# Four coupled edits to the order and the VectorE work of a two-kind attention stack on one Trainium2 core

## The chip, the cores and the metric

The kernel runs on one core of a Trainium2 chip. The metric is the time of one execution on the device in microseconds. TensorE (PE in the profile, its weight loads PEld), VectorE (DVE), ScalarE (ACT), GpSimd (POOL) and SyncE (SP, which here only issues DMAs) each run their own queue of instructions in order and wait for one another through semaphores.

## The reference

Four residual blocks on one sequence of 2048 rows by 512 columns, 32 heads of 16:

```python
def _A_ref(x, wqkv, wo):
    qkv = (x @ wqkv).reshape(B, S, 3, H, Dh).transpose(2, 0, 3, 1, 4)
    q, k, v = qkv[0], qkv[1], qkv[2]
    p = softmax(einsum("bhqd,bhkd->bhqk", q, k) * Dh ** -0.5)
    return einsum("bhqk,bhkd->bhqd", p, v).transpose(0, 2, 1, 3).reshape(B, S, D) @ wo

def _B_ref(x, wqkv, w_phi, wo):          # linear attention: phi has two softmaxes over 16
    ...
    num = einsum("bhqf,bhfd->bhqd", phi_q, kv)
    den = einsum("bhqf,bhf->bhq", phi_q, z)[..., None] + 1e-6
    return (num / den).transpose(0, 2, 1, 3).reshape(B, S, D) @ wo

x = x + _A_ref(layernorm(x), A_wqkv, A_wo)
x = x + _B_ref(layernorm(x), B_wqkv, B_w_phi, B_wo)
x = x + _A_ref(layernorm(x), A_wqkv, A_wo)
x = x + _B_ref(layernorm(x), B_wqkv, B_w_phi, B_wo)
```

The change concerns the two softmax attentions (`_A_ref`), called the first and the second attention here.

## The kernel before

**Groups, steps and tiles.** An attention is 32 groups: a group is four heads (`g`) and 512 queries (`j`). A group has 16 steps, one per 128 keys. A step needs two score tiles of 128 x 1024 (two heads each). `scores` (L1165 through `score_cols`) writes one into one of two PSUM buffers `s`; ScalarE exponentiates it into `p` (L1172), which has six buffers. When both tiles of a step are there, `pvs` (L1215) multiplies them with the values and adds into the group's accumulators, a pair of PSUM banks. There are two such pairs: `double` and `pm`. The other pair serves everything else that TensorE does on the side: projections for the next heads, output products, transposes for the next layer.

**End of a group.** `norm_task` empties the pair by two 32x32-block transposes on VectorE (`turned_sum`, L864, into tiles `yt` and `yb`), GpSimd adds the two halves (L867), VectorE takes the reciprocals (`rec`, L935 and L937) and scales (L942). Only the transposes keep the pair full. The names `vyt` are the same two transposes for values of later heads, `tq` (L887, L889) are queries and keys. `yt`, `vyt` and `tq` share one ring, the tag `yt`, of three tiles. A `vyt` tile leaves for the value buffer `v` by 16 DMAs on SP's queue (L877), and its slot is free when they have landed.

**An octet** is eight heads. While one octet is attended to, the values, queries and keys of the next are made: four value tiles, then eight query and key tiles, whose squares (`sq`, L982, on GpSimd) give norms; their maximum over all partitions is a GpSimd reduction (`nma`, L917) from VectorE's `nmx` (L914), and from it GpSimd computes a shift row `sh` and a check value `okt` (L921).

**Exponentials on VectorE.** Some score tiles do not go to ScalarE. `power_task` computes their exponential as a polynomial with VectorE: four instructions that empty the pair (L1183, L1186, into `px` and `pw`), and for each half a shift (L1192), a square `z = w * w` on GpSimd (`pz`, L1195) and four multiply-adds (L1197 to L1203). There is one buffer for such a tile (`px`). In the kernel before, it is always the second tile of a group's last step, at most one per group, and taken only after the group before has been finished.

**What sets the order.** The order on all compute engines is written out when the kernel is built. The loop in `attention` walks along TensorE's time by a table of costs (`UNIT` for a score tile or a side piece, `STEP` for a step's products, `EXP`, `THERE`, `BACK`) and picks what comes next: a score tile when a PSUM buffer and a `p` slot are due, a step's products, or a side piece. `Plan` keeps a clock for VectorE ("V") and GpSimd ("P"); tasks are generators that say which engine they need, for how long, and with which rank (lower first; 1 where none is given). `advance` gives each engine the due task of the lowest rank. These costs decide the order only; on the chip each queue runs when its waits are over. DMAs stand on SP's queue in the order in which tasks issue them.

At the end of the program VectorE and GpSimd reduce `okt` to a flag (`lowest` L1806, `bad` L1808, `anybad` L1810, `flag` L1812) that chooses a fallback; these four float to an earlier place in the queues.

## Time and profile before

| what | value |
|---|---|
| time, median of 3 runs (lowest to highest) | 2559.85 us (2557.07 to 2563.15) |
| profiled execution: its time, its span | 2557.37 us, 2555.6 us |
| mean granted TensorE clock | 0.983 |
| busy: PE, PEld, DVE, ACT, POOL | 2324.0, 1090.4, 1548.2, 2134.2, 633.0 us |
| first attention, from its first to past its last exponential | 71 to 1040 us |
| second attention | 1351 to 2305 us |

The rows of a group of instructions read: line, engine, operation, output<-inputs, shapes, count, then busy time and the mean of one in ns, then the idle time of the engine just before them with what ended most of it. Lines of waits read: who waited <- for whom: total us, times, longest. Timeline lines read: start and length in us, engine, line, operation, and in brackets the idle time before it. A wait for several semaphores is put down to the one that came last. SPq is SP's queue.

### The profile page before, as it was taken

How to read it: one execution, taken by the hardware profiler on the slowest of the kernel's cores; microseconds unless marked ns; L12 is line 12 of the kernel's file. 1: busy time of each engine (PE TensorE's matmuls, PEld its weight loads, DVE VectorE, ACT ScalarE, POOL GpSimd, SP SyncE). 2: the span in 40 equal slices, each digit the busy share in tenths (PEclk: the TensorE clock that was granted, in tenths of full speed). 3: DMA queues.
4: the chain of work that ended last, by engine and by line, in shares of the span. 5: the costliest groups of instructions: out<-in, count | busy, mean ns of one | idle time of the engine just before them, and what ended most of it. 6: DMA issues, size and time to landing. Idle time of an engine off the chain costs nothing.

```text
span 2555.6 us, 103557 instructions
## 1 busy us (share of the span) xinstructions
PE 2324.0 (91%) x46698; PEld 1090.4 (43%) x46698; DVE 1548.2 (61%) x2731; ACT 2134.2 (84%) x2382; POOL 633.0 (25%) x733
## 2 busy tenths in 40 slices
PE   6989999999989999899889999999899899998998
PEld 4434444444434444445344444444344344444543
DVE  8256556755556356789961565665465532468897
ACT  6889999999999999544438999999999999994553
POOL 3112211221121000366431122212122110005552
PEclk9999999999999999999899999999999999999999
DMA  5310331141036321000133003212300531110003
GB/s 194 64 26 7 74 63 33 51 56 43 3 93 167 127 85 60 26 17 17 67 102 55 16 16 46 39 24 35 58 3 11 94 110 61 61 68 26 9 18 109
DMA packets 114925, 142.86 MB, mean 56 GB/s; under 512 B 64184, under 2 KB 69928, under 8 KB 112168
## 3 DMA queue, kind: packets, MB, share of 16 engines
q1 hardware_dynamic: 113288, 133.38, 20.9%
q8 instruction: 367, 6.01, 1.0%
q0 software_dynamic: 1184, 2.77, 0.3%
q14 instruction: 86, 0.70, 0.1%
HBM read 62.16 MB, written 41.94 MB: 41 GB/s over the span
## 4 chain that ended last, share of the span: by engine, by line
ACT 44%; PE 24%; DVE 13%; issue 11%; SPq 5%; POOL 2%; DMA 1%; ACTq 0%; DVEq 0%; POOLq 0%
ACT p L1172 42%; PE double L1215 5%; PE s L1165 4%; SPq L877 3%; PE pm L699 2%; PE pm L1215 2%; PE pbv L1509 2%; DVE su L1579 1%; PE pk L1509 1%; PE po L682 1%; PE pq L1509 1%; SPq L1152 1%; DVE f L1571 1%; PE double L699 1%; DVE f L1572 1%
## 5 line engine op out<-in xcount | busy, mean ns | idle before, releaser
L1172 ACT ACTIVATE p<-s 128x1024 f32<-128x1024 f32 x2004 | 1851.4, 1067 | 72.5 <-PE s L1165 70.4
L1165 PE MATMUL s<-kq 49*32 49x512 f16 x15168 | 788.6, 382 | 103.4 <-ACT p L1172 90.4
L1165 PEld LDWEIGHTS <-kq 49*32 49x32 f16 x15872 | 386.8, 90 | 893.9 <-issue 822.6
L1215 PE MATMUL double<-p,v 64*32 64x512 f32 x10768 | 737.7, 591 | 12.1 <-DVE yt L864 6.3
L1215 PE MATMUL pm<-p,v 64*32 64x512 f32 x5264 | 359.9, 592 | 0.0
L867 POOL TENSOR_TENSOR yt<-yt,yt 128x512 f32<-128x512 f32 x64 | 83.5, 1304 | 772.4 <-DVE yt L864 719.5
L1215 PEld LDWEIGHTS double<-p,v 64*32 64x32 f32 x10768 | 207.9, 106 | 52.8 <-issue 13.7
L864 DVE STREAM_TRANSPOSE yt<-double 128x512 f32<-128x512 f32 x86 | 57.6, 698 | 222.5 <-PE double L1215 211.4
L1509 PEld LDWEIGHTS <-xnTa 128*128 128x128 f16 x1152 | 111.5, 99 | 156.9 <-DVE f L1572 28.1
L982 POOL TENSOR_TENSOR sq<-stg 128x512 bf16<-128x512 f16 x48 | 57.6, 1199 | 389.9 <-PE s L1165 278.6
L1588 POOL TENSOR_TENSOR f<-f,su 128x1024 f32<-128x1024 f32 x62 | 119.9, 1934 | 131.8 <-DVE su L1582 105.5
L1195 POOL TENSOR_TENSOR pz<-pw 128x512 f32<-128x512 f32 x88 | 99.6, 1137 | 92.4 <-DVE pw L1186 45.3
L1509 PE MATMUL pbv<-wbv,xnTa 128*128 128x512 f16 x384 | 95.4, 401 | 23.4 <-DVE f L1572 23.4
L1249 DVE SCALAR_TENSOR_TENSOR xt<-pm,c_oA,xt 128x512 f32<-128x512 f32 x68 | 50.5, 743 | 107.9 <-PE pm L699 105.8
L1573 ACT ACTIVATE f<-f,c_pB 128x1024 f32<-128x1024 f32 x64 | 72.7, 1148 | 50.4 <-DVE f L1572 50.3
L1197 DVE SCALAR_TENSOR_TENSOR px<-pz,px 128x512 f32<-128x512 f32 x88 | 78.8, 895 | 58.5 <-POOL pz L1195 51.6
L1215 PEld LDWEIGHTS pm<-p,v 64*32 64x32 f32 x5264 | 101.8, 106 | 17.8 <-DVE yt L864 1.8
L699 PEld LDWEIGHTS <-wA 64*32 64x32 f16 x4608 | 75.8, 93 | 42.2 <-issue 4.1
L1594 ACT ACTIVATE fk<-f 128x1024 f16<-128x1024 f32 x30 | 31.7, 1057 | 72.7 <-POOL f L1588 72.7
L864 DVE STREAM_TRANSPOSE vyt<-pm 128x512 f32<-128x512 f32 x46 | 30.2, 692 | 96.6 <-PE pm L699 83.5
L1509 PE MATMUL pq<-wbqk,xnTa 128*128 128x512 f16 x384 | 88.4, 379 | 0.0
L1509 PE MATMUL pk<-wbqk,xnTa 128*128 128x512 f16 x384 | 88.1, 379 | 0.0
(319 smaller groups left out, 3073.1 us busy)
## 6 DMA issues: line engine op xcount, KB each, us to landing
kq<-stg SPq DMA_DIRECT2D x168, 128.0 KB
xd<-xt SPq DMA_DIRECT2D x40, 512.0 KB
xt<-xd SPq DMA_DIRECT2D x40, 512.0 KB
v<-vyt SPq DMA_DIRECT2D x384, 16.0 KB
oD<-osp SPq DMA_DIRECT2D x24, 256.0 KB
ob<-oD SPq DMA_DIRECT2D x8, 768.0 KB
xt<-in_A_x_dram SPq DMA_DIRECT2D x8, 512.0 KB
wbqk<-dBqk SPq DMA_DIRECT2D x2, 2048.0 KB
```

The lines of the kernel that those rows point to most:

```text
L699: nc.tensor.matmul(ps[h][c, :], w[r, c], x[r], start=(n == 0), stop=(n == of - 1), skip_group_check=True)
L864: nc.vector.transpose(ys[u].rearrange("p a b -> p (a b)"), ps[u])
L867: nc.gpsimd.tensor_tensor(ys[0], ys[0], ys[1], ALU.add)
L877: nc.sync.dma_start(dst[:, :, 33 * a + 1:33 * a + 33], yt[32 * a:32 * a + 32, m:16:4, :])
L1165: nc.tensor.matmul(banks2[u][32 * c:32 * c + 32, :], self.side(g, half, 64 * u, 0, kt * P + 32 * c, 32), self.side(g, half, 64 * u, 1, j * ...
L1172: nc.scalar.activation(pt, s, AF.Exp, scale=EXPS)
L1195: nc.gpsimd.tensor_tensor(z, w, w, ALU.mult)
L1197: nc.vector.scalar_tensor_tensor(y, z, PB, y, op0=ALU.add, op1=ALU.mult)
L1215: nc.tensor.matmul(acc[h][32 * hh:32 * hh + 32, :], self.oct[o]["v"][r, x:x + 32], pt[r, hh % 2, :], start=(kt == 0), stop=(kt == NT - 1), ...
L1509: nc.tensor.matmul(dst, xnT[:, a, c, t * P:(t + 1) * P], w(b, c), start=(i == 0 and c == 0), stop=(i == 2 and c == NC4 - 1))
L1573: nc.scalar.activation(f, f, AF.Exp, scale=con["pB"])
L1588: nc.gpsimd.tensor_tensor(f3, f3, self.part_sums(f3, slice(0, 64), factor), ALU.mult)
```

## The change

- The transposes at a group's end get rank -1, and their task is announced one step's cost earlier. `advance` keeps an engine free for a task of negative rank that would become ready while another instruction runs.
- The square of the polynomial runs on VectorE, so that `power_task` uses no GpSimd.
- Any step's second tile may go to VectorE: the candidate is the second tile `LEAD` = 8 steps ahead of the next score tile. It is taken when the one `px` buffer and an accumulator pair are free, VectorE is booked for at most `VBUSY` = 0.4 us beyond now, the present group has at least three steps of products left, and its keys have landed by the plan (`landed`). It holds for groups 1 to 25.
- The ring `yt` gets four tiles, the ring `sq` four instead of five.
- Constants that set the order: `UNIT` 0.22 to 0.217, `STEP` 0.865 to 0.864, `THERE` 0.53 to 0.54, `BACK` 1.1 to 1.11, `POWERS` 24 to 26.

```diff
+LEAD = 8
+REST = 0.0
+VBUSY = 0.4
...
                     at = max(c, t.ready)
+                    for first in mine:
+                        if rank(first) < 0 and rank(t) >= 0 and max(c, first.ready) < at + t.need[1]:
+                            t, at = first, max(c, first.ready)
...
-        def turned_sum(self, idx, ps, name):
+        def turned_sum(self, idx, ps, name, rank=0):
...
-                yield "V", 0.68, 0
-                ys.append(np_.tile([P, 16, 32], F32, tag="yb" if u else "yt", name=name + str(u), bufs=2 if u else 3))
+                yield "V", 0.68, rank
+                ys.append(np_.tile([P, 16, 32], F32, tag="yb" if u else "yt", name=name + str(u), bufs=2 if u else 4))
...
-            yt = yield from self.turned_sum(idx, acc, "yt")
+            yt = yield from self.turned_sum(idx, acc, "yt", -1)
...
-                yield "P", 1.0
+                yield "V", 0.69, 2
                 z = new("pz")
-                nc.gpsimd.tensor_tensor(z, w, w, ALU.mult)
+                nc.vector.tensor_tensor(z, w, w, ALU.mult)
...
+                                if kt == NT - 1:
+                                    pvdone = G + 1
+                                    self.spawn(self.norm_task(G, idx, banks2), STEP + 0.3)
                                 pe += STEP
...
-                                if kt == NT - 1:
-                                    pvdone = G + 1
-                                    self.spawn(self.norm_task(G, idx, banks2))
                                 break
-                        if turn == 0 and tiles:
-                            G, kt, h = tiles[0]
-                            if tried < G and 0 < G < POWERS and pvdone >= G and kt <= 9 and min(self.pfree) <= pe and G in acc and pe + UNIT <= max(due, free):
-                                tried = G
-                                npow += 1
+                        if turn == 0 and tiles and pxfree <= pe and rested <= pe and plan.clock["V"] <= pe + VBUSY:
+                            n = NT * tiles[0][0] + tiles[0][1] + LEAD
+                            G, kt = n // NT, n % NT
+                            if 0 < G < POWERS and self.groups[G][0] in self.kq and plan.now >= self.landed[self.groups[G][0]] and pvq[0][0] in acc and \
+                               NT - pvq[0][1] >= 3 and min(self.pfree) <= pe and pe + UNIT <= max(due, free):
+                                power.add((G, kt, 1))
+                                pxfree, rested = FAR, pe + REST
                                 idx, ps = self.take()
-                                self.score_cols(*self.groups[G], NT - 1, 1, ps)
+                                self.score_cols(*self.groups[G], kt, 1, ps)
```

Lines behind the edits have other numbers in the changed kernel: L864, L867, L914, L935 and L1195 are L870, L873, L920, L941 and L1201 there.

What the change does to the queues, at three places. The first is VectorE's queue early in the first attention, from the third value tile of the second octet to the first tile of its keys (`tq`); `yt0_...` empties the accumulators of group 1. The brackets name what an instruction waits for; eight `DMAHW` names are the DMAs of a value tile that hold the ring's slot. Before:

```order
L864 STREAM_TRANSPOSE vyt0_1967<-pm0_1710 128x512 [waits DVE_49,PE_49]
L864 STREAM_TRANSPOSE vyt1_1969<-pm1_1711 128x512 [waits DMAHW4_49,DMAHW3_49,DMAHW5_49,DMAHW2_49,DMAHW6_49,DMAHW1_49,DMAHW7_49,DMAHW0_49,PE_49]
L864 STREAM_TRANSPOSE vyt0_2298<-pm0_1982 128x512 [waits DMAHW4_49,DMAHW3_49,DMAHW5_49,DMAHW2_49,DMAHW6_49,DMAHW1_49,DMAHW7_49,DMAHW0_49,PE_49]
L864 STREAM_TRANSPOSE vyt1_2300<-pm1_1983 128x512 [waits PE_49]
L887 TENSOR_SCALAR tq_2627<-pm0_2313,c_qk_359 128x512 [waits DMAHW4_49,DMAHW3_49,DMAHW5_49,DMAHW2_49,DMAHW6_49,DMAHW1_49,DMAHW7_49,DMAHW0_49,PE_49]
L889 SCALAR_TENSOR_TENSOR tq_2627<-pm1_2314,c_qk_359,tq_2627 128x512 [waits DVE_49,PE_49]
L864 STREAM_TRANSPOSE yt0_2641<-double_1907 128x512 [waits DMAHW3_49,DMAHW4_49,DMAHW2_49,DMAHW5_49,DMAHW1_49,DMAHW6_49,DMAHW0_49,DMAHW7_49,PE_49,Pool_49]
```

In the changed kernel, where a polynomial (sixteen rows, left out here) stands between the third and the fourth value tile:

```order
L870 STREAM_TRANSPOSE vyt0_2419<-pm0_2126 128x512 [waits PE_49]
L870 STREAM_TRANSPOSE vyt1_2440<-pm1_2127 128x512 [waits PE_49]
L870 STREAM_TRANSPOSE yt0_2610<-double_1871 128x512 [waits DMAHW4_49,DMAHW3_49,DMAHW5_49,DMAHW2_49,DMAHW6_49,DMAHW1_49,DMAHW7_49,DMAHW0_49,PE_49]
L870 STREAM_TRANSPOSE yt1_2639<-double_1871 128x512 [waits Pool_49]
L893 TENSOR_SCALAR tq_2683<-pm0_2453,c_qk_359 128x512 [waits DMAHW4_49,DMAHW3_49,DMAHW5_49,DMAHW2_49,DMAHW6_49,DMAHW1_49,DMAHW7_49,DMAHW0_49,PE_49]
```

The fourth value tile (`vyt0_2298` before, `vyt0_2419` now) waits for no DMA, and the emptying of group 1 stands ahead of the `tq` and waits for the DMAs of the first value tile instead of the third.

The second place is behind the reduction `nma` of the third octet in the first attention (values and keys for the third octet are made while the second is attended to). VectorE before:

```order
L914 TENSOR_REDUCE nmx_11427<-nm_7950 128x1 [waits DVE_49]
L1203 SCALAR_TENSOR_TENSOR px_11240<-pw_11273,px_11240 128x512 [waits DVE_49]
L1192 TENSOR_SCALAR px_11240<-px_11240 128x512
L1197 SCALAR_TENSOR_TENSOR px_11240<-pz_11579,px_11240 128x512 [waits DVE_49,Pool_49]
L1199 SCALAR_TENSOR_TENSOR pz_11579<-pw_11295,pz_11579 128x512 [waits DVE_49]
L1201 SCALAR_TENSOR_TENSOR px_11240<-pz_11579,px_11240 128x512 [waits DVE_49]
L1203 SCALAR_TENSOR_TENSOR px_11240<-pw_11295,px_11240 128x512 [waits DVE_49]
L864 STREAM_TRANSPOSE vyt0_11724<-double_11418 128x512 [waits PE_49]
```

VectorE now, up to the first instruction of the next polynomial:

```order
L920 TENSOR_REDUCE nmx_11579<-nm_7889 128x1 [waits DVE_49]
L870 STREAM_TRANSPOSE yt0_11677<-double_11011 128x512 [waits PE_49]
L870 STREAM_TRANSPOSE yt1_11706<-double_11011 128x512
L941 TENSOR_SCALAR rec_11786<-yt0_11677 128x16 [waits Pool_49]
L943 RECIPROCAL rec_11786<-rec_11786 128x16 [waits DVE_49]
L948 TENSOR_TENSOR yn_8984<-yt0_11677,rec_11786 128x16x16 [waits DVE_49]
L956 STREAM_TRANSPOSE yb_11839<-yn_8984 128x512 [waits DVE_49]
L959 CAST osp_11852<-yb_11839 128x512 [waits DMAHW7_49,DVE_49]
L870 STREAM_TRANSPOSE vyt0_11875<-pm0_11581 128x512 [waits PE_49]
L870 STREAM_TRANSPOSE vyt1_11885<-pm1_11582 128x512 [waits PE_49]
L1189 TENSOR_SCALAR px_11908<-pm0_11898 128x512 [waits PE_49]
```

GpSimd at the same place, before and now (an ISA row without names stands ahead of the reduction and again ahead of the next tensor instruction):

```order
L917 ISA nma_11438<-nmx_11427 128x1 [waits DVE_49]
L1195 ISA
L1195 TENSOR_TENSOR pz_11579<-pw_11295 128x512 [waits Pool_49]
L996 MEMSET sh_11600 1x512 [waits DMAHW6_49]
L921 TENSOR_SCALAR okt_134<-nma_11438 1x1 [waits Pool_49]
```

```order
L923 ISA nma_11591<-nmx_11579 128x1 [waits DVE_49]
L873 ISA
L873 TENSOR_TENSOR yt0_11677<-yt0_11677,yt1_11706 128x512 [waits DVE_49]
L1002 MEMSET sh_11780 1x512 [waits DMAHW6_49,Pool_49]
L927 TENSOR_SCALAR okt_134<-nma_11591 1x1 [waits Pool_49]
```

The instruction behind the reduction on GpSimd was the polynomial's square and is now the sum of a finished group's halves; VectorE's `rec` waits for it where `px` did. The same exchange stands behind the reductions of the third and fourth octet in the second attention.

The third place is VectorE behind the last reduction of the second attention, where the program's flag has floated to. Before:

```order
L1197 SCALAR_TENSOR_TENSOR px_41487<-pz_41754,px_41487 128x512 [waits DVE_49,Pool_49]
L1806 TENSOR_REDUCE lowest_51803<-okt_134 32x1 [waits Pool_49]
L1199 SCALAR_TENSOR_TENSOR pz_41754<-pw_41578,pz_41754 128x512 [waits DVE_49]
L1808 TENSOR_SCALAR bad_51805<-lowest_51803 32x1 [waits DVE_49]
L1201 SCALAR_TENSOR_TENSOR px_41487<-pz_41754,px_41487 128x512 [waits DVE_49]
L1203 SCALAR_TENSOR_TENSOR px_41487<-pw_41578,px_41487 128x512 [waits DVE_49]
L1812 CAST flag_51809<-anybad_51807 32x1 [waits Pool_49]
L864 STREAM_TRANSPOSE yt0_41957<-double_41431 128x512 [waits PE_49]
```

Now:

```order
L920 TENSOR_REDUCE nmx_41903<-nm_38607 128x1 [waits DVE_49]
L870 STREAM_TRANSPOSE yt0_41967<-double_41343 128x512 [waits PE_49]
L870 STREAM_TRANSPOSE yt1_41990<-double_41343 128x512
L1818 TENSOR_REDUCE lowest_51861<-okt_134 32x1 [waits Pool_49]
L1820 TENSOR_SCALAR bad_51863<-lowest_51861 32x1 [waits DVE_49]
L1189 TENSOR_SCALAR px_42012<-double_42003 128x512 [waits PE_49]
```

The group's transposes stand ahead of `lowest` and of the flag now, and a polynomial's first instruction stands behind `lowest`.

More of the change, by code (lines that the diff above doesn't have):

```diff
@@ L51 @@
 FAR = 1e9
[L52 to L53 removed]
+UNIT = 0.217
+STEP = 0.864
 EXP = 0.904
[L55 to L57 removed]
+THERE = 0.54
+BACK = 1.11
+POWERS = 26
+LEAD = 8
+REST = 0.0
+VBUSY = 0.4
 LATE = 0.15
@@ L1360, in attention @@
                 plan.add(extra[1], 0.0)
+            self.landed = {0: 0.0, 1: 40.0}
             def pairs(g):
@@ L1364, in pairs @@
                 self.load_pairs(g)
+                self.landed[g] = plan.now + 16.0
             events = []
@@ L1375, in attention @@
             pe = act = 0.0
-            tried = -1
-            npow = 0
+            power, pxfree, rested = set(), 0.0, 0.0
             lost = 0.0
@@ L1465, in attention @@
             assert not plan.tasks and not events
-            print("attention", self.li, "powers", npow, round(pe, 1), "exponentials", len(estart), "late", round(lost, 1), "ready", self.ready)
+            print("attention", self.li, "powers", len(power), round(pe, 1), "exponentials", len(estart), "late", round(lost, 1), "ready", self.ready)
             self.fill.append(self.last_tail(NJ - 1, self.last))
```

23 lines of the change are left out of this document (10 added, 13 removed).

## The prediction

> **What bounds the kernel now.** I read the head of the page, its chain and the line of the exponentials first, then the busy time of each engine in the two attention stretches, then the waits. In the group line the last part is the idle time of ScalarE in front of these instructions and what ended it; in the two lines of stretches the columns are the length, then the busy time of PE, PEld, DVE, ACT and POOL.
>
> ```profile
> span 2555.6 us, 103557 instructions
> ACT 44%; PE 24%; DVE 13%; issue 11%; SPq 5%; POOL 2%; DMA 1%; ACTq 0%; DVEq 0%; POOLq 0%
> L1172 ACT ACTIVATE p<-s 128x1024 f32<-128x1024 f32 x2004 | 1851.4, 1067 | 72.5 <-PE s L1165 70.4
> 71.00:1040.00 969.00, 898.60 (x21460) 409.34 (x21464) 532.14 (x960) 926.66 (x1002) 163.99 (x155) 0.99 0.26 62
> 1351.00:2305.00 954.00, 882.63 (x21373) 400.48 (x21367) 482.79 (x843) 924.72 (x1002) 161.82 (x148) 1.00 0.21 46
> ACT p L1172 <- PE s L1165: 70.4, 65, 7.5
> ```
>
> The two attentions are 1923 of 2556 us, and ScalarE's exponentials fill 96 and 97% of them. An exponential costs 1851.4 / 2004 = 0.924 us. What is left is 70.4 us in which ScalarE waits, 65 times, for TensorE to deliver scores. TensorE runs its queue in order, so whatever holds TensorE up shows there. VectorE is half idle (437 and 471 us). The change acts on these stretches alone; the rest of the span has the same instructions. It can therefore gain by fewer exponentials and by shorter waits, at most 72.5 us for the latter. I looked up what ended the largest ones.
>
> Ring of transposed tiles: the windows 138 to 152 and 592 to 600 (who waited for whom: total, times, longest).
>
> ```profile
> 108.36 35.49 SPq L877 DMA_DIRECT2D v<-vyt  x48
> 134.40 0.75 DVE L887 TENSOR_SCALAR tq<-pm,c_qk 128x512 f32<-128x512 f32 x1 [10.64 <-DMA v<-vyt]
> 145.28 0.72 DVE L864 STREAM_TRANSPOSE yt<-double 128x512 f32<-128x512 f32 x1 [8.90 <-DMA v<-vyt]
> PE double L1165 <- DVE yt L864: 7.7, 1, 7.7
> ACT p L1172 <- PE s L1165: 9.1, 3, 7.5
> ...
> DVE tq L887 <- DMA v<-vyt: 4.4, 1, 4.4
> ACT p L1172 <- PE s L1165: 4.0, 2, 3.3
> ```
>
> A value tile leaves by 16 DMAs, 35.49 / 3 = 11.8 us of SP's queue, and holds its slot of the ring until the last has landed. With three slots VectorE stands in front of the next `yt` or `tq`, an accumulator pair stays full, TensorE waits for it, and ScalarE loses 9.1 and 4.0 us.
>
> GpSimd's square in the polynomial: window 1540 to 1564, and the totals.
>
> ```profile
> 1543.35 0.15 DVE L914 TENSOR_REDUCE nmx<-nm 128x1 f32<-128x4 f32 x1
> 1547.36 0.38 POOL L917 PARTITION_ALL_REDUCE nma<-nmx  x1 [5.83 <-issue]
> 1554.55 1.03 POOL L1195 TENSOR_TENSOR pz<-pw 128x512 f32<-128x512 f32 x1 [6.82 <-issue]
> 1555.62 0.69 DVE L1197 SCALAR_TENSOR_TENSOR px<-pz,px 128x512 f32<-128x512 f32 x1 [10.40 <-POOL pz L1195]
> PE pm L699 <- DVE vyt L864: 2.7, 2, 2.5
> ACT p L1172 <- PE s L1165: 2.8, 1, 2.8
> ...
> DVE px L1197 <- POOL pz L1195: 51.6, 6, 13.5
> ```
>
> After the cross-partition maximum GpSimd does nothing for 6.82 us, and before it 5.83; its next tensor instruction starts 11.1 us after `nmx`. VectorE waits 10.4 us for the square, the transposes of a value tile queue behind it, and TensorE waits for their accumulators. Windows 1727 to 1744 and 1981 to 1986 show the same chain, the second with the end-of-kernel flag (L1812) behind it as well; in 520 to 536 a like wait costs ScalarE next to nothing, since nothing urgent is queued behind it:
>
> ```profile
> ACT p L1172 <- PE s L1165: 4.3, 2, 3.2
> ...
> DVE px L1197 <- POOL pz L1195: 8.6, 1, 8.6
> ACT p L1172 <- PE s L1165: 0.4, 1, 0.4
> ...
> 1981.82 0.14 DVE L1812 CAST flag<-anybad 32x1 int32<-32x1 f32 x1 [5.85 <-POOL anybad L1810]
> ACT p L1172 <- PE s L1165: 2.4, 1, 2.4
> ```
>
> Group boundaries: an ordinary one, and who waits for L864.
>
> ```profile
> 1653.38 1.31 DVE L864 STREAM_TRANSPOSE yt<-double 128x512 f32<-128x512 f32 x2 [6.42 <-PE double L1215]
> 1654.84 1.09 PE L1215 MATMUL double<-p,v 64*32 64x512 f32 x16 [0.17 <-PE pm L699]
> 1656.26 4.69 ACT L1172 ACTIVATE p<-s 128x1024 f32<-128x1024 f32 x5 [0.64 <-PE s L1165]
> ...
>   PE double L1215: 211.4, 37
>   PE pm L1215: 75.2, 16
> ...
>   PE double L1215: 6.3, 6
> ```
>
> While the two transposes empty the pair, TensorE fills in other work and then has two steps to catch up; ScalarE loses 0.64 us. The named waits sum to 9.1 + 4.0 + 2.8 + 4.3 + 2.4 = 22.6; the other 57 waits hold 70.4 - 22.6 = 47.8 us, 0.84 each, most of them such boundaries.
>
> **The change part by part.**
>
> *Tiles anywhere.* The order has 96 `pz` rows instead of 88: 48 tiles for VectorE instead of 44. Four exponentials fewer are 4 x 0.924 = 3.7 us. Ends: 0 and 3.7.
>
> *Longer ring.* At the first place of the order shown above, the change puts `yt0_2610`, which empties group 1, ahead of the `tq` and on the slot of the first value tile. That tile's sixteen DMAs are issued by 108.36 + 11.8 = 120.2, 14 us before even the `tq` of before starts; the wait of 8.9 us has nothing left. Around 595 the `tq` that waited falls on a `yt` slot, free by then. I take 9.1 + 4.0 = 13.1. Ends: 0 (SP's queue is no shorter, and the wait only moves on) and 13.1.
>
> *Polynomial without GpSimd.* The waits of 2.8, 4.3 and 2.4 us can't occur in that form: 9.5 us. Ends 0 and 9.5. The square itself moves to VectorE: 96 instructions. The trace has no such product there; the nearest rows are these, all of 128x512 f32.
>
> ```profile
> L1195 POOL TENSOR_TENSOR pz<-pw 128x512 f32<-128x512 f32 x88 | 99.6, 1137 | 92.4 <-DVE pw L1186 45.3 <-issue 37.8 <-DVE rec L935 5.9
> L647 DVE TENSOR_TENSOR yn<-yt,rec 128x512 f32<-128x512 f32 x32 | 22.7, 711 | 0.0
> L1197 DVE SCALAR_TENSOR_TENSOR px<-pz,px 128x512 f32<-128x512 f32 x88 | 78.8, 895 | 58.5 <-POOL pz L1195 51.6 <-DVE px L1192 0.5
> L1199 DVE SCALAR_TENSOR_TENSOR pz<-pw,pz 128x512 f32<-128x512 f32 x88 | 64.8, 737 | 2.5
> ```
>
> By 0.711 us (between 0.711 and 0.895) that is 68 us, and four more tiles of 10.9 us (below) are 44: 112 us into 908 us of idle VectorE. On the path: nothing, as long as a tile is ready when its step comes (third rival).
>
> *What takes the GpSimd slot.* The reductions stay. At three of them (third octet of the first attention, third and fourth of the second) the order now has the `yt` sum of a finished group right behind the reduction on GpSimd, where `pz` stood, and VectorE's `rec` waits for that sum, with value transposes or a score tile behind it. At the third, VectorE's `lowest` waits for `okt`, which comes after that sum. So a wait of some 5 to 10 us returns at three places. The waits of before that were 8.6 us and longer cost ScalarE between 0.4 and 4.3 us; I take 3 each, 9 us, nearer to those with an emptying behind them, as here. Ends: 3 x 0.4 = 1 and 3 x 4.3 = 13.
>
> *Transposes first.* They start the moment the pair is full at 37 + 16 = 53 of 64 boundaries already; rank can only help the other eleven, by a VectorE instruction of about 0.7 us or two, and TensorE waited directly 6.3 us in six places. By the order the next group takes the same pair at 48 of 62 boundaries (44 before), so the 1.31 us of transposing itself stays. A score tile for VectorE no longer always fills a group's last step, which eases some boundaries more. I take 10 of the 47.8 us, nearest to the 6.3 that the trace shows. Ends: 0 and 47.8. What VectorE idles while it holds itself free for a transpose lies in its idle half.
>
> *The rest.* `sq` with four slots instead of five: a set of four is consumed before the next is written, 0. The DMAs are the same ones, a few places earlier or later on SP, 0. The new constants only set the order.
>
> Sum, against the profiled execution of 2557.4: -3.7 - 13.1 - 9.5 + 9 - 10 = -27.3, so 2530. That execution lies 2.5 us under the median of the runs, 2559.9; beside the median the forecast is **2532 us**. TensorE is idle for 70 us of each stretch, so taking some 14 us from each does not make it the bound.
>
> **The rivals.**
>
> *More of it* (0.16): the three new waits fall where nothing urgent is queued, like that in 520 to 536, and the boundaries give 20: -3.7 - 22.6 + 1 - 20 = -45, 2512, or 2514 beside the median. For it: the boundaries hold 47.8 us. Against it: they keep their 1.31 us.
>
> *The waits change hands* (0.17): the new waits cost 13, and the boundaries give nothing, since the transposes were in time at 53 of 64: -3.7 - 22.6 + 13 = -13, 2544, or 2547 beside the median.
>
> *Late polynomials, slower* (0.10): a tile's place used to be the last step of its group, taken many steps ahead; now it is 8 steps after the start. A step lasts 969 / 512 = 1.89 us, and the products trail by about two tiles: some 17 us of room. A polynomial needs 4 x 0.68 + 2 x (0.50 + 0.71 + 0.74 + 0.74 + 0.72 + 0.71) = 10.9 us from these rows and those above:
>
> ```profile
> L1183 DVE TENSOR_SCALAR px<-pm 128x512 f32<-128x512 f32 x60 | 40.5, 675 | 5.4 <-PE pm L1165 5.2
> L1186 DVE SCALAR_TENSOR_TENSOR pw<-px,pm 128x512 f32<-128x512 f32 x60 | 40.7, 679 | 1.1
> L1192 DVE TENSOR_SCALAR px<-px 128x512 int32<-128x512 int32 x88 | 44.2, 502 | 0.0
> L1201 DVE SCALAR_TENSOR_TENSOR px<-pz,px 128x512 f32<-128x512 f32 x88 | 63.7, 724 | 2.7
> L1203 DVE SCALAR_TENSOR_TENSOR px<-pw,px 128x512 f32<-128x512 f32 x88 | 62.7, 713 | 2.8
> ```
>
> VectorE's other work is (532 - 22 x 9.5) / 969 = 33%, so 5.6 of the 17 us: 16.5 needed. If the tiles come late, TensorE stands in front of them. The gain of 27 is gone at 27 / 48 = 0.57 us per tile; at 1 us the time is 2532 + 48 = 2580. Against it: a tile is only started when VectorE is nearly free, and the exponentials' six slots cover part of a wait. [...]
>
> *It does not do what it says* (0.07): only the four tiles change hands: 2556.
>
> **How the numbers follow.** The forecast has 0.50, its own range 2520 to 2543. The range that should hold 8 of 10 reaches from the first rival to just short of the fourth: 2512 to 2557. A measurement of this kernel tells about 0.2%, 5 us, from no change. Faster: 0.50 + 0.16 + 0.13 of the second rival = 0.79; same: its other 0.04 and the fourth = 0.11; slower 0.10.
>
> **What would show it.** Exponentials 2000; ScalarE's idle time in front of them near 45 us instead of 72.5; no VectorE wait on `v<-vyt` over 3 us at the first octet; no `px` wait on GpSimd, but three `rec` or `lowest` waits of 4 to 10 us behind a reduction, with a ScalarE gap of about 3 us each. TensorE waiting for `px` (L1209) at several tiles would show the slow rival. The forecast is wrong if the attentions are not shorter by 10 to 17 us each, or if the time comes from elsewhere.

## The result, and the profile after

The changed kernel takes 2528.11 us (median of four runs, 2526.15 to 2529.67) against 2558.46 us before (2556.27 to 2563.15): a ratio of 0.9879, 95% interval 0.9861 to 0.9896, or 31 us less (27 to 36). (A fourth run of the kernel before stands beside the three of the first table, so its median is 2558.46 here.) The forecast was 2532, with 2512 to 2557 as its range. The profiled execution took 2528.14 us.

Head of the page of the changed kernel, its chain, the group line of the exponentials, its two attention stretches (from the first exponential to the end of the last one) and ScalarE's largest wait:

```profile
span 2526.1 us, 103429 instructions
ACT 51%; PE 20%; DVE 13%; issue 12%; POOL 3%; SPq 1%; DMA 1%; ACTq 0%; POOLq 0%; DVEq 0%
L1178 ACT ACTIVATE p<-s 128x1024 f32<-128x1024 f32 x2000 | 1846.5, 1068 | 47.6 <-PE s L1171 46.1
71.00:1025.90 954.90, 893.63 (x21456) 410.22 (x21455) 557.51 (x1020) 925.11 (x1001) 114.03 (x111) 1.00 0.27 63
1338.70:2275.50 936.80, 880.81 (x21360) 400.19 (x21359) 528.09 (x935) 921.30 (x999) 113.98 (x104) 1.00 0.22 47
ACT p L1178 <- PE s L1171: 46.1, 55, 4.8
```

The span is 29.5 us shorter. Four exponentials fewer are 3.7 us, and ScalarE's idle time in front of the others has gone from 72.5 to 47.6 us, 24.9 less: 28.6 of the 29.5. By the same measure the attentions took 968.5 and 953.0 us before: they are 13.6 and 16.2 us shorter, and the rest of the span is 634 us as it was. VectorE works 25 and 45 us more in them, GpSimd 50 and 48 us less, and neither is the bound.

What VectorE waits for in the changed kernel (waits of the whole span; then single rows of its timeline at the four places named below, with the idle time ahead in brackets):

```profile
DVE rec L941 <- POOL yt L873: 39.5, 20, 7.0
DVE lowest L1818 <- POOL okt L927: 7.3, 1, 7.3
DVE tq L893 <- DMA v<-vyt: 6.0, 2, 3.4
...
429.31 0.38 POOL L345 PARTITION_ALL_REDUCE sAo_mm<-sAo_m  x1 [5.85 <-issue]
437.12 1.25 POOL L873 TENSOR_TENSOR yt<-yt,yt 128x512 f32<-128x512 f32 x1 [7.43 <-issue]
438.40 0.17 DVE L941 TENSOR_SCALAR rec<-yt 128x16 f32<-128x16 f32 x1 [7.01 <-POOL yt L873]
530.14 0.47 DVE L941 TENSOR_SCALAR rec<-yt 128x16 f32<-128x16 f32 x1 [6.26 <-POOL yt L873]
1728.99 0.47 DVE L941 TENSOR_SCALAR rec<-yt 128x16 f32<-128x16 f32 x1 [1.93 <-POOL yt L873]
```

No `px` waits for GpSimd any more. The waits on `v<-vyt` are down to 6.0 us from 26.6 + 11.1 = 37.7, as these rows of the kernel before have it:

```profile
DVE tq L887 <- DMA v<-vyt: 26.6, 3, 11.5
DVE yt L864 <- DMA v<-vyt: 11.1, 2, 8.9
```

In their place `rec` waits for the sum of a group's halves, where that sum stands behind a reduction on GpSimd: the reduction at 429 is followed by 7.43 us in which GpSimd does nothing, then by the sum. Two of these waits reach ScalarE (windows 430 to 445 and 526 to 540):

```profile
ACT p L1178 <- PE s L1171: 6.6, 3, 4.8
PE pm L1171 <- DVE tq L895: 4.8, 1, 4.8
...
ACT p L1178 <- PE s L1171: 5.2, 4, 3.3
PE pm L1171 <- DVE vyt L870: 3.4, 2, 3.1
```

The other two, around 1729 and the `lowest` at 1961, cost ScalarE 1.4 and 1.2 us in their windows, not more than an ordinary boundary or two.

### The profile page after: what moved, and what is told of

It is laid out like the page before. It is cut to its first block, busy times and chain, and to the rows that moved or that the text cites. A ratio compares the mean times of both kernels' runs of the same rounds, so it can differ in the third digit from the quotient of the medians.

```text
span 2526.1 us, 103429 instructions
## 1 busy us (share of the span) xinstructions
PE 2314.9 (92%) x46698; PEld 1090.1 (43%) x46698; DVE 1618.7 (64%) x2883; ACT 2129.0 (84%) x2378; POOL 535.2 (21%) x645
## 3 DMA queue, kind: packets, MB, share of 16 engines
q1 hardware_dynamic: 113288, 133.38, 21.5%
## 4 chain that ended last, share of the span: by engine, by line
ACT 51%; PE 20%; DVE 13%; issue 12%; POOL 3%; SPq 1%; DMA 1%; ACTq 0%; POOLq 0%; DVEq 0%
ACT p L1178 49%; PE s L1171 4%; PE double L1221 4%; PE pm L1221 2%; DVE su L1591 2%; PE pm L702 2%; PE po L685 1%; PE pbv L1521 1%; PE pk L1521 1%; POOL f L1600 1%; DVE f L1583 1%; SPq L883 1%; DVE f L1584 1%; DVE mx L1580 1%; PE pq L1521 1%
## 5 line engine op out<-in xcount | busy, mean ns | idle before, releaser
L1178 ACT ACTIVATE p<-s 128x1024 f32<-128x1024 f32 x2000 | 1846.5, 1068 | 47.6 <-PE s L1171 46.1
L1221 PE MATMUL double<-p,v 64*32 64x512 f32 x8984 | 617.1, 592 | 2.4 <-DVE yt L870 1.1
L1221 PE MATMUL pm<-p,v 64*32 64x512 f32 x7016 | 479.6, 589 | 0.3 <-issue 0.3
L873 POOL TENSOR_TENSOR yt<-yt,yt 128x512 f32<-128x512 f32 x64 | 87.4, 1365 | 863.2 <-DVE yt L870 809.3
L1221 PEld LDWEIGHTS double<-p,v 64*32 64x32 f32 x8984 | 175.0, 106 | 32.1 <-PE pm L702 3.8
L1221 PEld LDWEIGHTS pm<-p,v 64*32 64x32 f32 x7016 | 136.0, 106 | 24.6 <-issue 2.2
L870 DVE STREAM_TRANSPOSE yt<-double 128x512 f32<-128x512 f32 x72 | 47.3, 696 | 131.5 <-PE double L1221 131.5
L1255 DVE SCALAR_TENSOR_TENSOR xt<-pm,c_oA,xt 128x512 f32<-128x512 f32 x52 | 38.9, 748 | 100.3 <-PE pm L702 87.5
L1255 DVE SCALAR_TENSOR_TENSOR xt<-double,c_oA,xt 128x512 f32<-128x512 f32 x60 | 44.8, 747 | 89.4 <-PE double L702 88.7
L1591 DVE TENSOR_REDUCE su<-f 128x64 f32<-128x1024 f32 x64 | 77.5, 1211 | 9.5 <-ACT f L1585 8.9
L1203 DVE SCALAR_TENSOR_TENSOR px<-pz,px 128x512 f32<-128x512 f32 x96 | 74.0, 771 | 2.7
```

What stands on the lines that cost most here:

```text
L873: nc.gpsimd.tensor_tensor(ys[0], ys[0], ys[1], ALU.add)
L1178: nc.scalar.activation(pt, s, AF.Exp, scale=EXPS)
L1203: nc.vector.scalar_tensor_tensor(y, z, PB, y, op0=ALU.add, op1=ALU.mult)
L1221: nc.tensor.matmul(acc[h][32 * hh:32 * hh + 32, :], self.oct[o]["v"][r, x:x + 32], pt[r, hh % 2, :], start=(kt == 0), stop=(kt == NT - 1), ...
L1255: nc.vector.scalar_tensor_tensor(xt[:, u, :], ps[h], con["oA"], xt[:, u, :], op0=ALU.mult, op1=ALU.add)
L1591: nc.vector.tensor_reduce(su, f[:, r, :], AX.X, ALU.add)
```

## The experiments

All were timed beside the kernel before on the same chip; the ratios are to it. To compare them on one scale I multiply ratios with 2558.5 us: a difference between two ratios of 0.001 is 2.6 us, and a difference of two kernels from different comparisons is uncertain by 5 to 6 us. "Idle" is ScalarE's idle time in the group line of the exponentials. "Long" is the part of it in waits of 2.3 us or more, with those of 0.9 us or more within the 6 us behind them; "rest" is what remains. The three come from one profiled execution of each kernel.

| kernel | median us | ratio (95%) | exps | idle | long | rest |
|---|---|---|---|---|---|---|
| before | 2558.46 | 1 | 2004 | 72.5 | 21.5 | 51.0 |
| changed | 2528.11 | 0.9879 (0.9861 to 0.9896) | 2000 | 47.6 | 9.2 | 38.4 |
| e1 ring alone | 2547.64 | 0.9944 (0.9930 to 0.9957) | 2004 | 62.7 | 13.3 | 49.4 |
| e2 ring undone | 2549.12 | 0.9954 (0.9941 to 0.9968) | 2000 | 76.0 | 34.5 | 41.5 |
| e3 square on GpSimd | 2573.34 | 1.0049 (1.0035 to 1.0063) | 2000 | 90.9 | 53.6 | 37.3 |
| e4 sums on VectorE | 2513.49 | 0.9813 (0.9800 to 0.9826) | 2000 | 34.7 | 0.0 | 34.7 |
| e5 polynomial alone | 2550.97 | 0.9958 (0.9941 to 0.9974) | 2005 | 64.6 | 19.9 | 44.7 |
| e6 ranks undone | 2538.64 | 0.9907 (0.9891 to 0.9924) | 1998 | 53.4 | 12.0 | 41.4 |
| e7 old places | 2534.06 | 0.9892 (0.9875 to 0.9909) | 2004 | 49.6 | 0.0 | 49.6 |
| e8 sums booked | 2520.50 | 0.9840 (0.9822 to 0.9858) | 1999 | 37.2 | 4.1 | 33.1 |
| e9 old places, GpSimd square | 2552.58 | 0.9959 (0.9944 to 0.9973) | 2004 | 68.4 | 12.4 | 56.0 |
| e10 ring and polynomial | 2536.82 | 0.9903 (0.9886 to 0.9920) | 2005 | 56.8 | 10.9 | 45.9 |
| e11 LEAD 9 | 2541.54 | 0.9915 (0.9898 to 0.9932) | 2002 | 58.0 | 18.7 | 39.3 |
| e12 LEAD 9, sums on VectorE | 2520.65 | 0.9856 (0.9831 to 0.9880) | 2002 | 38.1 | 2.4 | 35.7 |

### The ring

e1, on the kernel before (the order stays as it was; `sq` goes to four slots as in the change):

```diff
-  ... tag="yb" if u else "yt", ..., bufs=2 if u else 3)
+  ... tag="yb" if u else "yt", ..., bufs=2 if u else 4)
-  tq = np_.tile([P, 512], F32, tag="yt", name="tq", bufs=3)
+  tq = np_.tile([P, 512], F32, tag="yt", name="tq", bufs=4)
```

> The kernel before with the longer ring of transposed tiles alone (four yt slots, four sq slots). The order of every queue stays as it was; only the slots differ. Theory (the ring's waits are a term of their own, 13 us): VectorE's waits of 8.9 and 4.4 us on the DMAs of value tiles go, ScalarE's idle time in front of the exponentials falls from 72.5 to about 59 us, the time by 11 to 13 us (ratio 0.995). Rival (SP's queue is no shorter, so the wait only moves one tile on): less than 3 us.

14.3 us less (11 to 18), slightly above the theory's 11 to 13. ScalarE's waits at 148 (7.5 and 1.1 us) and 598 (3.3) are gone, and VectorE waits 2.2 us for `v<-vyt` in all where it waited 37.7. ScalarE's idle time fell by 9.8 us only, to 62.7 where 59 was expected: the long waits of the second attention are 13.3 us now, 3.7 more than before.

e2, on the changed kernel, the same lines with 3 for 4.

> The changed kernel with three yt slots again, order unchanged. Theory: the group's transposes come first now and wait about 2 us for the second value tile, the first tq then waits some 10 us for the third; 5 to 13 us slower than the changed kernel, 2533 to 2541 us. Rival (the ring only matters in the order of before): at most 3 us slower.

19 us more than the changed kernel, above both expectations. Waits of VectorE, then of TensorE, in the whole span of e2:

```profile
DVE tq L893 <- DMA v<-vyt: 18.4, 2, 9.8
DVE vyt L870 <- DMA kq<-sh: 8.8, 1, 8.8
DVE yt L870 <- DMA v<-vyt: 6.0, 1, 6.0
PE pm L1171 <- DVE tq L893: 16.5, 3, 8.1
```

The two places are those of before, at 148 and 611, but ScalarE loses 9.2 + 1.1 and 7.9 + 1.1 us there, not 9.1 and 4.0: at both the `tq` on the slot is now late enough that TensorE waits 8.1 and 6.9 us for it. (The 8.8 us in the second line, at 337, held up neither TensorE nor ScalarE.) So the ring seems worth more under the changed order, 19.3 us against 13.1 at the two places; by the times, 19 and 14 can't be told apart. (This profiled execution took 2558.7 us, 9.5 above its median, so its idle time of 76.0 overstates the middle.)

### The polynomial and the room of its tiles

e5, on the kernel before, with the order laid out for it:

```diff
-                yield "P", 1.0
+                yield "V", 0.69, 2
-                nc.gpsimd.tensor_tensor(z, w, w, ALU.mult)
+                nc.vector.tensor_tensor(z, w, w, ALU.mult)
```

> The kernel before with one edit: the square of the polynomial goes to VectorE, in the code and in the plan (L1195 and the 1.0 us booked for it). Theory: the six long px waits behind GpSimd's pz (51.6 us of VectorE's idle time, of which 9.5 us reached ScalarE) go, and the 9.5 us with them; the one urgent sum that now stands straight behind a reduction gives some 2 to 4 us back: 6 to 9 us faster, 2551 to 2555 us, with ScalarE's idle time in front of its exponentials at 63 to 67 us instead of 72.5. Rival (the order): a square that VectorE does shifts the order of the whole attention, the new waits outweigh the old ones, and the time is the one before or worse, 2558 to 2568 us. Second rival (more of it): the squares cost far more than their waits show, and the time falls by over 15 us, below 2545 us.

10.7 us less (7 to 15), a little beyond the theory. The waits of 2.8, 3.2 + 1.1 and 2.4 us in the second attention are gone. A new one stands at 450, where the sum of a group falls behind the reduction of L342 (waits in the window 438 to 457 of e5):

```profile
ACT p L1172 <- PE s L1165: 7.2, 2, 6.1
DVE sAo_mm L344 <- POOL sAo_mm L342: 5.6, 1, 5.6
DVE rec L935 <- POOL yt L867: 4.6, 1, 4.6
```

So the edit won 9.5 us at the places named and lost most of that at a new one; what is left over lies in smaller waits (51.0 to 44.7). The new order also has 43 tiles on VectorE instead of 44.

e3, on the changed kernel, at an unchanged order:

```diff
-                nc.vector.tensor_tensor(z, w, w, ALU.mult)
+                nc.gpsimd.tensor_tensor(z, w, w, ALU.mult)
```

> The changed kernel with the polynomial's square issued on GpSimd again, at the same place of the written order (the plan still books it on VectorE). Theory: at the reductions of the second octets and at four others the square stands behind GpSimd's idle stretch again, VectorE waits 5 to 10 us for it at four places; with 0.4 to 4.3 us of ScalarE each the kernel is 4 to 12 us slower than the changed one, 2532 to 2540. [...] Rival (late polynomials): TensorE waits for px at many tiles, 20 us or more slower.

43 us more than the changed kernel: the theory missed it by a factor of four, and the rival of late polynomials came true in size, though TensorE waits for a polynomial at three tiles, not at many. ScalarE's idle time rose by 43.3 us, all of the loss. Waits of TensorE and VectorE in e3, then one tile in its timeline:

```profile
PE double L1221 <- DVE px L1209: 14.4, 2, 8.2
PE pm L1221 <- DVE px L1209: 7.8, 2, 6.4
DVE px L1203 <- POOL pz L1201: 50.1, 9, 13.2
...
732.89 1.03 POOL L1201 TENSOR_TENSOR pz<-pw 128x512 f32<-128x512 f32 x1 [8.72 <-issue]
733.96 0.69 DVE L1203 SCALAR_TENSOR_TENSOR px<-pz,px 128x512 f32<-128x512 f32 x1 [13.19 <-POOL pz L1201]
736.13 1.06 DVE L1209 SCALAR_TENSOR_TENSOR px<-pw,px 128x512 f32<-128x512 f32 x1
737.25 1.07 PE L1221 MATMUL double<-px,v 64*32 64x512 f32 x2 [8.24 <-DVE px L1209]
```

Before, six such waits summed to 51.6 us of VectorE and cost ScalarE 9.5. Here nine sum to 50.1, and TensorE itself stands in front of the product with the tile. The difference is the room: the time from a tile's last polynomial instruction to TensorE's first product with it. I took it for each tile from the start and end of these rows. Before, half of the 44 tiles have over 11.5 us, and the longest 15.4; in the changed kernel half of the 48 have over 5.7, and the longest 9.5. Some tiles have none left, and the products with their first half begin before the second half is done: by 0.5 us at two tiles of the kernel before (at 529 and 738, behind two of the six late squares), by 1.3 us at one of the changed kernel (at 1973). At 1555 the kernel before has a `px` wait of 10.40 us (shown in the prediction), and its products start 5.5 us after the polynomial all the same:

```profile
1557.79 1.06 DVE L1203 SCALAR_TENSOR_TENSOR px<-pw,px 128x512 f32<-128x512 f32 x1
1564.40 0.60 PE L1215 MATMUL double<-px,v 64*32 64x512 f32 x4
```

e9 tells whether the room decides: the old places for the tiles, and the square on GpSimd. It is set against e7 (below), which has the old places and the square on VectorE.

> Two edits on the changed kernel: the old rule for VectorE's tiles, and the square of the polynomial on GpSimd at an unchanged order. In the traces so far the time from a tile's last polynomial instruction to TensorE's product with it is about 4 to 17 us (half of them over 11) under the old rule and 0.2 to 9.5 us (half of them over 5.6) under the new one, and a pz that stands behind a reduction on GpSimd comes about 9 to 13 us late. Theory (the slack decides what a late square costs): with the old places the same late squares are hidden for the most part, and the square on GpSimd adds 3 to 14 us to the kernel with the old places, not 43: 2537 to 2548 us. [...]

17 us more than e7, just above the room's expectation and far under the 43 us of e3. The square's waits on GpSimd are as long as in e3, but TensorE no longer waits for a polynomial. ScalarE's idle time is 18.8 us above e7's, 12.4 of it in two places, where other work of VectorE queues behind `px`, as before; the rest is spread over small waits. The waits in the whole span of e9, then TensorE's at the second of these places:

```profile
DVE px L1203 <- POOL pz L1201: 59.7, 9, 11.1
...
PE pm L702 <- DVE vyt L870: 4.8, 1, 4.8
```

So of the 43 us late squares cost 17 with the long room of the old places, and about 26 more (uncertain by some 8 us) with the short room of the new ones. The trace of e3 has a like split: at three of its long waits, 32 us with what follows them, TensorE waits for a polynomial; at two, 11 us, for transposes queued behind one. The polynomial without GpSimd is what makes the new places affordable; neither of the two edits is to be priced without the other.

### Ranks and places

e6, on the changed kernel (the task that empties the sums also starts where it did before):

```diff
-            for first in mine:
-                if rank(first) < 0 and rank(t) >= 0 and max(c, first.ready) < at + t.need[1]:
-                    t, at = first, max(c, first.ready)
-            yt = yield from self.turned_sum(idx, acc, "yt", -1)
+            yt = yield from self.turned_sum(idx, acc, "yt", 0)
-                                    self.spawn(self.norm_task(G, idx, banks2), STEP + 0.3)
+                                    self.spawn(self.norm_task(G, idx, banks2))
```

> The changed kernel without the rank of the transposes and without the early start of the task that empties the sums; tiles, ring and polynomial stay as changed. Theory (the ranks shorten the changes from group to group): TensorE waits again for yt (1.5 us at some group ends) and the small boundary waits of 0.6 to 1.5 us come back, of which the change had taken about 15 us: slower than the changed kernel by 8 to 15 us, 2536 to 2543 us. Rival (tiles): the small waits went because VectorE's tiles now lie at other places, not through the ranks; undoing the ranks moves less than 4 us, 2524 to 2532 us. Second rival (the new waits come from the ranks): the transposes that now go first are what brings the sums behind reductions, and without them the 12 to 15 us of rec waits go: faster, 2512 to 2520 us.

e7, on the changed kernel:

```diff
-  if turn == 0 and tiles and pxfree <= pe and rested <= pe and plan.clock["V"] <= pe + VBUSY:
-      n = NT * tiles[0][0] + tiles[0][1] + LEAD
-      ...
+  if turn == 0 and tiles:
+      G, kt, h = tiles[0]
+      if (G, NT - 1, 1) not in power and 0 < G < 24 and pvdone >= G and kt <= 9 and ...:
+          kt = NT - 1
```

> The changed kernel with the old rule for VectorE's tiles (second half of a group's last tile, or an early tile of the group): the order then has 44 tiles on VectorE as before, not 48. Theory: four exponentials of 0.924 us come back to ScalarE and little else moves: slower by 3 to 8 us, 2531 to 2536 us. Rival (tiles carry the boundaries): the small waits in front of the exponentials come back with the old places: slower by 12 to 20 us, 2540 to 2548 us. Second rival: the old places keep VectorE free where the reductions end, and it is faster than the changed kernel, below 2525 us.

By the ratios e6 is 7 us slower than the changed kernel and e7 3 us, each within the uncertainty of such a difference or at its edge: e6 lies between its theory and its rival (its median, 2538.6, inside the theory), and e7 at the low end of its theory. The traces say more. Who waited for the transposes of L870 in front of the next group's products, in the changed kernel, in e7 and in e6 (there L867); before it was 6.3 us in six places:

```profile
  PE double L1221: 1.1, 2
```

```profile
  PE double L1221: 6.5, 9
```

```profile
  PE double L1218: 1.3, 1
  PE pm L1218: 1.0, 3
```

With the ranks and the old places TensorE waits as before; without the ranks and with the new places it waits 2.3 us. The table's last column says the same with all kernels: 45 to 56 us of small waits in the six kernels with the old places (before, e1, e5, e7, e9, e10), 33 to 42 us in the eight with the new ones. The small waits that lie within 8 us behind the end of a group (the start of its transposes), sorted by whether the group's last step has a VectorE tile, show why:

| kernel | ends with a tile: ScalarE's small waits | ends without |
|---|---|---|
| before | 44 ends, 28.8 us, 0.65 each | 20 ends, 6.8 us, 0.34 each |
| e7 old places, with the ranks | 44 ends, 26.3 us, 0.60 each | 20 ends, 6.0 us, 0.30 each |
| changed | none | 64 ends, 22.5 us, 0.35 each |
| e6 new places, without the ranks | 1 end, 0.0 us | 63 ends, 25.7 us, 0.41 each |

A tile in the last step costs some 0.3 us more, ranks or not, and the changed kernel has none there: 44 x 0.3 is the 13 us by which the boundaries gained. So it is the places that eased the boundaries; the ranks give some 3 us at most, by one execution each. The ranks do what they are for: VectorE already waits for the pair when it fills at 64 of 64 ends in the changed kernel and 63 in e7, against 55 in e6 and 53 before. But that was not what held TensorE up. How a tile in the last step adds its 0.3 us is not shown; a busy VectorE it is not in e7. e7 loses so little because it also has none of the long waits: 11.2 us more in small ones, 9.2 less in long ones.

e10, the kernel before with the edits of e1 and e5 together:

> The kernel before with two of the four edits: the ring of four tiles, and the square of the polynomial on VectorE in code and plan; no ranks, old places. Theory (the two gains, 14 and 11 us alone, add up, and ranks with new places give the remaining 5 us of the change's 30): 2531 to 2537 us. Rival (each hides a part of the other, so that ranks and places give 10 to 15 us together): 2538 to 2544 us. Second rival (the ranks and places give nothing, their new waits eat them): 2524 to 2530 us.

24.8 us less, and 14.3 + 10.7 = 25.0: the two add up. The other 6 us of the change are left for ranks, places and the new constants together, as the theory had it, but that is no more than the uncertainty of the difference. The constants were not run alone.

e11, on the changed kernel: no instruction of another kind, but another layout.

```diff
-LEAD = 8
+LEAD = 9
```

> The changed kernel with LEAD = 9 instead of 8: a VectorE tile is chosen one score tile further ahead, and the order is laid out anew, with no instruction added or changed. It measures what a new layout alone moves. Theory (which sums fall behind a reduction is chance): some of the three new waits go and others come, with 0 to 16 us of rec waits that reach ScalarE, and the time lies between 2512 and 2536 us; ScalarE's idle time outside these waits stays at 35 to 41 us. Rival (the new places fix the waits): the same three waits at the same reductions, 2525 to 2531 us.

9 us slower than the changed kernel; the time, 2541.54, is 5 us beyond the theory's upper end (by the ratio 2537). The rest of the idle time, 39.3, stayed as forecast, and the long waits doubled, to 18.7: two stand at the same reductions as in the changed kernel, as the rival had it, and two new ones at 800 and 922, where the layout put more sums behind reductions. The layout also has 46 tiles on VectorE, not 48, so that two more exponentials, 1.8 us, go to ScalarE.

```profile
DVE rec L941 <- POOL yt L873: 51.6, 25, 7.3
...
797.63 0.17 DVE L941 TENSOR_SCALAR rec<-yt 128x16 f32<-128x16 f32 x1 [3.80 <-POOL yt L873]
919.29 0.17 DVE L941 TENSOR_SCALAR rec<-yt 128x16 f32<-128x16 f32 x1 [4.08 <-POOL yt L873]
```

A constant that changes only the layout moves the time by as much as undoing the ranks or the places. That is the size of what can't be told from the times of e6 and e7.

### The sums behind reductions

e4, on the changed kernel at an unchanged order. Seven sums that the plan has within 13 us behind a reduction go to VectorE:

```diff
+            soon = rank < 0 and self.plan.now < state["red"] + 13.0
-            nc.gpsimd.tensor_tensor(ys[0], ys[0], ys[1], ALU.add)
+            (nc.vector if soon else nc.gpsimd).tensor_tensor(ys[0], ys[0], ys[1], ALU.add)
```

(`state["red"]` is the plan's time of the last reduction, set behind the two lines that issue one.)

> The changed kernel with the sum of a finished group's two halves issued on VectorE instead of GpSimd where it falls within 13 us of the plan behind a GpSimd reduction (seven sums); the written order is otherwise the same. Theory (what the change gave back is this sum behind the reduction): the waits of rec of 7.0, 6.3, 1.9 and 3.3 us go, ScalarE's idle time falls from 47.6 to about 35, the time by 9 to 13 us, to 2515 to 2519. Rival (those gaps have another cause, the accumulators or TensorE's own queue): within 3 us of the changed kernel.

15 us less than the changed kernel by the medians (17 by the ratios), slightly more than forecast. The exponentials' line of e4, its two kinds of sums, and the place of the first wait:

```profile
L1181 ACT ACTIVATE p<-s 128x1024 f32<-128x1024 f32 x2000 | 1845.6, 1068 | 34.7 <-PE s L1174 33.1
L875 POOL TENSOR_TENSOR yt<-yt,yt 128x512 f32<-128x512 f32 x57 | 78.0, 1368 | 798.9 <-DVE yt L871 784.1 <-DMA v<-vyt 14.7
L875 DVE TENSOR_TENSOR yt<-yt,yt 128x512 f32<-128x512 f32 x7 | 4.8, 683 | 0.0
429.71 0.38 POOL L346 PARTITION_ALL_REDUCE sAo_mm<-sAo_m  x1 [5.85 <-issue]
432.31 0.16 DVE L944 TENSOR_SCALAR rec<-yt 128x16 f32<-128x16 f32 x1
```

Seven additions of 0.683 us on an engine with idle time take the place of the waits: `rec` starts 2.6 us after the reduction where it started 9.1 us after it, no long wait is left, and ScalarE's idle time falls by 12.9 us. At 2513.5 us this kernel beats both.

e8 books the same sums on VectorE in the plan and lets it lay out the order anew:

> The changed kernel with the urgent sums behind a reduction on VectorE, as in the run with seven such sums at an unchanged order, but booked on VectorE in the plan, so that the order is laid out for it. Theory (the 12 to 15 us of the new waits go and the order is as good as before): 2508 to 2518 us. Rival (a new order is a new draw): another layout brings other small waits, 2520 to 2532 us, which would say that an edit at an unchanged order is worth more than a planned one.

10 us less than the changed kernel by the ratio. The time, 2520.5, is at the lower end of the rival's range, and by the ratio, 2517.5, inside the theory's: the run doesn't decide between them. Counted from the first exponential to the last, its attentions are 946.4 + 932.9 = 1879.3 us, e4's 942.5 + 935.1 = 1877.6: as good. The other 9 us by which its span is longer lie in the stretches around the attentions, in that one execution; why is open.

e12 is e11 with the edit of e4:

> The kernel with LEAD = 9, with the urgent sums that stand close behind a reduction moved from GpSimd to VectorE at an unchanged order, as was done with the changed kernel. With LEAD = 9 five rec waits stood behind reductions and 18.7 us of them reached ScalarE in seven long waits; the time was 2541.5 us. Theory (what a new layout costs or gives is which sums fall behind reductions): the long waits go and with them 15 to 21 us, 2520 to 2527 us, and the two layouts, 13 us apart before, stand within 12 us of each other (the changed kernel with the same edit: 2513.5 us). Rival (layouts differ by more than these waits): under 10 us are won, 2532 us or more.

15 us less than e11 by the ratios, 21 by the medians; the long waits are down from 18.7 to 2.4 us:

```profile
L1181 ACT ACTIVATE p<-s 128x1024 f32<-128x1024 f32 x2002 | 1847.8, 1068 | 38.1 <-PE s L1174 35.7 <-ACT p L1181 0.4
DVE rec L944 <- POOL yt L875: 29.3, 21, 3.6
```

So the long waits of that layout, too, were sums behind reductions, and the same edit is worth about as much there as in the changed kernel (15 and 17 us by the ratios). What sets the layout back against the changed kernel's is not settled by it: the two stood 9 us apart by the ratios and 13 by the medians, and with the sums moved they stand 11 and 7 apart.

## Why the prediction was right, point by point

*Bound.* ScalarE's exponentials, held up by TensorE, held up by VectorE: 28.6 of the 29.5 us of the span came from fewer exponentials and shorter waits in front of them, and none from outside the attentions. They are 13.6 and 16.2 us shorter, where 10 to 17 were expected.

*Tiles anywhere, -3.7.* 2000 exponentials, as forecast. But the step saw only the exponentials in this edit. Its places carry the boundaries too (below).

*Longer ring, -13.1.* Both waits are gone; alone the ring gave 14.3. The expected sign, no wait on `v<-vyt` over 3 us at the first octet, is there: 2.5 us at 136. Right under either order in kind; under the changed order undoing it costs 19.

*Polynomial without GpSimd, -9.5.* The three waits are gone and alone it gave 10.7, including a new wait behind another reduction. The square on VectorE was priced at 0.711 us and takes 0.691:

```profile
L1201 DVE TENSOR_TENSOR pz<-pw 128x512 f32<-128x512 f32 x96 | 66.3, 691 | 0.0
L1203 DVE SCALAR_TENSOR_TENSOR px<-pz,px 128x512 f32<-128x512 f32 x96 | 74.0, 771 | 2.7
```

*What takes the GpSimd slot, +9.* The mechanism was right, the places and sizes were not. Of the three places named, the one in the first attention cost ScalarE 5.2 us in its window; the two in the second cost 1.4 and 1.2, ordinary boundaries included. A fourth, 6.6 us at 438, was missed: it stands behind the reduction of L345, in the preparation of the output weights, and the prediction took only the reductions of L923. The four windows hold 14.4 us, and e4, in which these waits are gone, has 12.9 us less idle time. By that the term was mis-sized by about 4 us, from a missed place and from one price for all.

*Transposes first, -10 at the boundaries.* The small waits fell from 51.0 to 38.4 us, 12.6 less, so the size is close; the reason given is not. The step that failed is "rank can only help the other eleven ... I take 10", with the 6.3 us of direct waits as its measure: with the ranks and the old places TensorE waits 6.5 us for the transposes, without the ranks and with the new places 2.3, and the small waits behind the group ends are 3 us apart with and without the ranks. The remark beside it, that a score tile for VectorE no longer always fills a group's last step, was the one that counted: it holds some 13 us.

The two errors offset each other. If the new waits are 12.9 us, as e4 has it, the rest of the idle time fell from 72.5 - 22.6 = 49.9 to 34.7, by 15.2 where 10 was taken: +4 at the reductions, -5 at the boundaries. That the sum came within 4 us of the time is in part luck.

*The rivals.* "More of it" had the boundaries at 20 and the new waits at 1: neither came. Taking the waits away by e4 gives its time, 2513.5 against 2514, though not its terms. "The waits change hands" had the new waits right (13) and the boundaries wrong. "Late polynomials" did not come: TensorE waited once, for 0.3 us.

```profile
PE pm L1221 <- DVE px L1209: 0.3, 1, 0.3
```

The margin is not large: the room was put at 17 us with 16.5 needed, and the trace has 5.7 left in the middle and none at that one tile. e3 takes it away with a square some 10 us late at a few tiles, and the loss is 43 us. No run shows the 1 us a tile in that rival's 2580 as a price that each of 48 tiles pays: in e3 five late tiles cost 4 to 12 us each, and the others nothing.

## What to carry to other kernels

An engine that is idle most of the time (GpSimd, busy 114 of 955 us in the first attention) can still be a poor place for a short urgent step, if anything slow stands in its queue (here the reduction at 429, with `rec` 9.1 us behind it): look at what lies ahead of the step there, and move the step, not the whole work; seven additions moved were worth 15 us. Price an edit that shortens a buffer of time together with those that use it: late squares cost 17 us with 11.5 us of room and 43 with half of it. And where an order is laid out by a planner, change a constant that should not matter to see what a new layout alone moves (here 9 us) before a few us are ascribed to an edit; a trace whose waits are sorted by length and by place still tells edits apart when the times don't.

## What of the hardware was not expected

A square on GpSimd lengthened the VectorE instruction that ran beside it: in e9 an L1203 took 1.34 us at 741.86, where GpSimd squares until 742.66, and another 0.69 us at 716.12, where GpSimd is idle. Group lines of L1203 in e7 (square on VectorE) and in e9 (square on GpSimd), otherwise the same order:

```profile
L1203 DVE SCALAR_TENSOR_TENSOR px<-pz,px 128x512 f32<-128x512 f32 x88 | 60.8, 691 | 2.6
```

```profile
L1203 DVE SCALAR_TENSOR_TENSOR px<-pz,px 128x512 f32<-128x512 f32 x88 | 83.4, 948 | 66.7 <-POOL pz L1201 59.7
```

948 ns against 691, 37% more, where the prediction's rows have 895 against 737 for two different lines (L1197 and L1199). Here it is 88 x 0.257 = 23 us of VectorE in all. How much of it reaches ScalarE was not separated from the late squares.

GpSimd stands still on both sides of the reduction at 429, 5.85 us ahead of it and 7.43 behind (rows at 429 and 437). The profile puts both down to `issue`; what holds GpSimd there, no trace here shows. The second stretch, ahead of the next tensor instruction, is the longer one here, and it is the one that the sum waits for.
